# Start-up of a fused retention and MLP kernel: v's first cast on ScalarE, g zeroed and loaded later, fillers cut short, a quarter of w1 loaded earlier

## The chip, the cores and the metric

The kernel runs on one core of a Trainium2 chip. The metric is the device time of one execution in microseconds (us), as the median of several. Most executions of one kernel agree within some 0.3%. Experiments were timed in five rounds beside the kernel before, on the same chip; two were only looked at with a profile. What is discussed is the ratio and its 95% interval. A run is called slow when it is over 1.5% above the fastest of its kernel.

## The reference

```python
# attention part, B, H, S, D = 4, 8, 768, 64
gamma = 1.0 - 2.0 ** (-5.0 - np.arange(H))
for t in range(S):
    state = gamma * state + einsum('bhd,bhe->bhde', k[:, :, t], v[:, :, t])
    y[:, :, t] = scale * einsum('bhd,bhde->bhe', q[:, :, t], state)
x = y.transpose(0, 2, 1, 3).reshape(B, S, H * D)          # 4 x 768 x 512
# MLP part
xn = (x - mean(x)) / sqrt(var(x) + 1e-6) * g_ln
out = x + maximum(xn @ w_ch1, 0) @ w_ch2                  # w_ch1 512 x 2048, w_ch2 2048 x 512
```

## The kernel before

The four sequences are cut into 24 tiles of 128 positions. In the texts below, q(1) is q of tile 1, py(0) the output of tile 0, and so on; g is `g_ln` of the reference, which is needed on all 128 partitions. For a tile, TensorE transposes k and q ("tk", "tq"), makes the scores ("pa") and the output ("py"). VectorE masks the scores and normalises the output to xn. TensorE transposes xn ("tx") and multiplies it by w1 in four quarters for each of the first tiles ("products", line 589); ScalarE or VectorE applies the ReLU. The second matrix product (line 626) follows much later.

A planner inside the kernel decides the order on each engine when the program is built. It holds an estimated duration for each task and takes the task that can start earliest, then the one of lowest rank. Its numbers are estimates that set an order; the chip then runs that fixed order, each engine waiting where data are not there.

The parts that the change touches:

```python
    def c_small(eng):
        nc.vector.memset(zeros, 0.0)
        nc.vector.memset(grow, 0.0)          # 128 x 512, only row 0 is then loaded
        ...
    small = a(DVE, 1450, -100, c_small)      # engine, ns, rank, what to emit
    ...
    maskd = a(DVE, 1230, -50, c_mask, [vscd, tri])
    ...
    def c_gb(eng):                           # g on all partitions: ones^T x grow
        p = take("mm", "g", [P, DM], FP32)
        nc.tensor.matmul(p, lhsT=ones, rhs=grow, start=True, stop=True)

    grd = a(SP, 390, -150, lambda eng: nc.sync.dma_start(
        out=grow[0:1, :], in_=moe_g_ln.rearrange("(o n) -> o n", o=1)), [small], lat=4500)
    gbm = a(PE, 1000, 12, c_gb, [grd, small2], ("mm", "g"), at=7600)
    ...
            if j == 0:                       # tile 0 comes as fp32 and is cast
                loaded[kind, j] = a({"k": {ACT: 620}, "q": {DVE: 490}, "v": {ACT: 620, DVE: 430}}[kind], ...)
    ...
    # GpSimd issues the other loads; a load waits for the one eight places ahead of it
    first = ["iota", "pos", "k1", "q1", "v1", "w1_0", "k2", "q2", "w1_1", "v2", "k3", "q3", "v3",
             "w1_2", "k4", "q4", "v4", "w1_3", "k5", "q5", "v5"]
    ...
    def warm(n):                             # fillers: matmuls on zeros while TensorE would idle
        if ("mm", "warm") not in held:
            take("mm", "warm", [P, GMAX * P], FP32)      # pool "mm" has two buffers
        for w in [GMAX * P] * (n // GMAX) + [P] * (n % GMAX):
            nc.tensor.matmul(held["mm", "warm"][:, 0:w], lhsT=zeros[:, 0:P], rhs=zeros[:, 0:w], ...)
    ...
        for t in plan.fill(plan.order(), PE, 1100, 20000, lambda at: 110 if at < 11500 else 80, warm):
            t["emit"](t["eng"])              # fillers up to 20000 planned ns
```

Of the kernel before, what the change touches and what calls it, by code (L numbers as in the profile page):

```python
# [14 lines left out]
PE, ACT, DVE, POOL, SP = range(5)  # L15
# [101 lines left out]
def kernel(  # L117
# [16 lines left out]
    nc = tc.nc  # L134
# [25 lines left out]
    plan = Plan({PE: 330, ACT: 130, DVE: 130, POOL: 130, SP: 0},  # L160
                {PE: 900, ACT: 800, DVE: 900, POOL: 850, SP: 800}, 2300, 8, 5300)
# [21 lines left out]
    def take(pool, key, shape, dtype):  # L183
        held[pool, key] = pools[pool].tile(shape, dtype, name=pool, tag=pool)
        return held[pool, key]

    def evacuate(eng, dst, src):
        nc.scalar.copy(out=dst, in_=src) if eng == ACT else nc.vector.tensor_copy(out=dst, in_=src)
# [18 lines left out]
    pos = const.tile([P, C, H], FP32, name="pos")  # L207
# [3 lines left out]
    grow = const.tile([P, DM], FP32, name="grow")  # L211
# [5 lines left out]
    w2 = const.tile([P, HO, DM], BF16, name="w2")  # L217
    x_all = const.tile([P, NT, DM], BF16, name="x_all")

    def c_small(eng):  # L220
        nc.vector.memset(zeros, 0.0)  # L221
        nc.vector.memset(grow, 0.0)
        for i in range(NPAIR):
            nc.vector.memset(lgq[0:D, i:i + 1], lngam[2 * i])
            nc.vector.memset(lgq[D:P, i:i + 1], lngam[2 * i + 1])
        nc.vector.memset(ln8, math.log(scale))
        for h in range(H):
            nc.vector.memset(lgh[:, :, h], lngam[h])
# [43 lines left out]
            nc.gpsimd.memset(x, 0.0)  # L272

    a = plan.add
    small = a(DVE, 1450, -100, c_small)
    small2 = a(DVE, 200, -99, c_small2)
    iota = a(POOL, 250, 0, c_iota)
    ipos = a(POOL, 250, 0, c_pos)
# [14 lines left out]
    def c_gb(eng):  # L293
# [1 line left out]
        nc.tensor.matmul(p, lhsT=ones, rhs=grow, start=True, stop=True)  # L295

    grd = a(SP, 390, -150, lambda eng: nc.sync.dma_start(
        out=grow[0:1, :], in_=moe_g_ln.rearrange("(o n) -> o n", o=1)), [small], lat=4500)
    gbm = a(PE, 1000, 12, c_gb, [grd, small2], ("mm", "g"), at=7600)
    gl = a(ACT, 600, -40, lambda eng: nc.scalar.copy(out=gb, in_=held["mm", "g"]), [gbm],  # L300
           uses=[("mm", "g")])
# [3 lines left out]
    loaded, where = {}, {}  # L305

    def tile_of(kind, t):
        if kind != "v" and t >= T0:
            return held["qk", t][:, "qk".index(kind)]
        return held[where[kind, t]]  # L310

    def load(kind, j, rank):
        takes, uses, follows = None, [], []
        if kind in "qkv":
            b, c = TILES[j]
            src = {"q": q, "k": k, "v": v}[kind][b].rearrange("h (c p) d -> c p h d", p=P)[c]
            ns, dma = 910, 900
            pair = kind != "v" and j >= T0
            name = "qk" if pair else kind + ("0" if c == 0 and kind != "q" else "sb")
            takes = where[kind, j] = (name, j)  # L320
            if pair and kind == "q":
                takes, uses, follows = None, [takes], [loaded["k", j]]

            if j == 0:

                def emit32(eng):
                    dst = take("osb", kind, [P, DM], FP32).rearrange("p (h d) -> p h d", d=D)
                    (nc.scalar if eng == ACT else nc.sync).dma_start(out=dst, in_=src)
                raw = a(ACT if kind == "q" else SP, 390, -200 + "kqv".index(kind), emit32, (),
                        ("osb", kind), (), 0, {"k": 3400, "q": 4000, "v": 4800}[kind])  # L330

                def emit(eng):
                    evacuate(eng, take(*takes, [P, H, D], BF16),
                             held["osb", kind].rearrange("p (h d) -> p h d", d=D))
                loaded[kind, j] = a({"k": {ACT: 620}, "q": {DVE: 490}, "v": {ACT: 620, DVE: 430}}[kind], 0, -60, emit,
                                    [raw], takes, [("osb", kind)])
                return

            def emit(eng):
                if takes:  # L340
                    take(*takes, [P, 2, H, D] if pair else [P, H, D], BF16)
                nc.gpsimd.dma_start(out=tile_of(kind, j), in_=src)  # L342
        else:
            s = slice(j * DM, (j + 1) * DM)
            o = slice(j * KO, (j + 1) * KO)
            src, dst = (w1_v[:, :, s], w1[:, :, s]) if kind == "w1" else (w2_v[:, o, :], w2[:, o, :])
            ns, dma = 820, 2450 if kind == "w1" else 2800

            def emit(eng):
                nc.gpsimd.dma_start(out=dst, in_=src)  # L350
        loaded[kind, j] = a(POOL, ns, rank, emit, (), takes, uses, dma,
                            4000 if kind in "qkv" and j > 7 else 1400 if late(kind, j) else 500,
                            follows=follows)

    def late(kind, j):
        return j > 2 if kind in "qkv" else kind == "w2" or j > 0


    first = ["iota", "pos", "k1", "q1", "v1", "w1_0", "k2", "q2", "w1_1", "v2", "k3", "q3", "v3",
             "w1_2", "k4", "q4", "v4", "w1_3", "k5", "q5", "v5"]  # L360
    pool_rank = {x: i - 1000 for i, x in enumerate(first)}
    seq = [(x, t) for t in range(8) for x in "kqv"] + [("w1", j) for j in range(4)]
    seq += [("w2", j) for j in range(4)] + [(x, 8) for x in "kqv"]
# [1 line left out]
    for i, (x, j) in enumerate(seq):  # L365
        load(x, j, pool_rank.get(f"{x}_{j}" if x[0] == "w" else f"{x}{j}", 20 * i))
# [25 lines left out]
    for t in range(NT):  # L392
        b, c = TILES[t]
# [97 lines left out]
        if c > 0:  # L491
            for cc in ([0, 1] if c == 1 else [c]):
                if cc == C - 1:
                    continue
                j = number[b, cc]

                def e_vg(eng, j=j, cc=cc):
                    e = nc.gpsimd if eng == POOL else nc.vector
                    e.tensor_tensor(  # L499
                        out=take("vg", j, [P, H, D], BF16), in0=tile_of("v", j),  # L500
                        in1=vsc[:, cc, :].unsqueeze(2).to_broadcast([P, H, D]), op=ALU.mult)
                vgt = a(POOL, 1050, -500 if j == 4 else r - 2 if cc == 0 else r + 1, e_vg,
                        [loaded["v", j], vscd] + vgs[-1:], ("vg", j), [where["v", j]],
                        lat=2500 if j > 7 else 0,
                        follows=[loaded["q", j + 2]] if T0 <= j < NT - 2 else [])
                vgs.append(vgt)

                def e_pd(eng, j=j, b=b, cc=cc):
                    if cc == 0:
                        take("pd", b, [P, NPAIR, P], FP32)  # L510
                    for i in range(NPAIR):
                        nc.tensor.matmul(  # L512
                            held["pd", b][:, i, :], lhsT=tile_of("k", j)[:, 2 * i:2 * i + 2, :],
                            rhs=held["vg", j][:, 2 * i:2 * i + 2, :],
                            start=(cc == 0 and i == 0), stop=(cc == C - 2), skip_group_check=True)
                pdt = a(PE, 230, r - 1 if cc == 0 else r + 2.2, e_pd,
                        [vgt, loaded["k", j]] + ([pbt[j]] if cc else []),
                        ("pd", b) if cc == 0 else None,
                        [("vg", j), where["k", j]] + ([("pd", b)] if cc else []), at=0 if cc or b else 20000)

                def e_pb(eng, n=number[b, cc + 1], b=b, cc=cc):

                    held["pb", n] = state[len(pbs) % 2]
                    pbs.append(n)
                    for o in (slice(0, D), slice(D, P)):
                        nc.vector.tensor_tensor(  # L526
                            out=held["pb", n][o, :, o], in0=held["pd", b][o, :, o],
                            in1=gch[o, cc, :].unsqueeze(2).to_broadcast([D, NPAIR, D]), op=ALU.mult)
                pbt[number[b, cc + 1]] = a(
                    DVE, 690, r - 1 if cc == 0 else r + 4, e_pb, [pdt, gchd, zerod],  # L530
                    ("pb", number[b, cc + 1]), [("pd", b)])
                if cc == 0:

                    pyt["after"].append(pbt[t])
# [43 lines left out]
    for g in range(NG):  # L578
        n = GROUPS[g]
        hb, h0 = buf_of[g]  # L580
        two = GMAX // n
        for ho in range(0, HO, two):
# [22 lines left out]
            first = ho == 0 and h0 == 0  # L605
# [45 lines left out]
                             start=True, stop=True)  # L651

    with tc.manual_schedule():
        for t in plan.fill(plan.order(), PE, 1100, 20000, lambda at: 110 if at < 11500 else 80, warm):
            t["emit"](t["eng"])


# [28 lines left out]
```

## Time and profile before

| | kernel before |
|---|---|
| median of 3 runs | 215.68 us (215.56 to 215.99) |
| span in the profile | 213.7 us |
| TensorE busy | 96% of the span, 7.95 us of it fillers |
| VectorE, ScalarE, GpSimd busy | 57%, 38%, 42% |
| first product starts | 13.56 us |

In a profile line of the timeline the columns are: start, length (both us), engine, source line, operation with output and inputs, count, and in brackets the idle time just ahead of it with what ended it. One more reading of the kernel before, from VectorE's timeline:

```profile
6.83 0.43 DVE L188 CAST v<-osb 128x512 bf16<-128x512 f32 x1 [0.74 <-DMA osb<-in_v_dram]
7.17 0.42 DVE L416 TENSOR_TENSOR trq<-tp,qsc 128x512 bf16<-128x512 bf16 x1
```

The first part of the change aims at this cast.

### The profile page before, as it was taken

The numbers are of one execution on the slowest core, as the hardware profiler recorded it, in microseconds if no ns is written. First come the engines' busy times: TensorE is split into PE (matmuls) and PEld (weight loads), VectorE is DVE, ScalarE is ACT, GpSimd is POOL, SyncE is SP. The second block draws the span as 40 slices with busy tenths as digits, with TensorE's granted clock in tenths as the row PEclk, the third lists the DMA queues.
The fourth block names the chain that finished last, engine by engine and source line by source line (L and its number), as shares of the span: only waits on it lengthen the run. The fifth ranks groups of instructions, "written<-read, shape, count | busy, mean of one in ns | idle before, by whom it ended". The sixth has DMA issues, their size and how long they took to land.

```text
span 213.7 us, 4698 instructions
## 1 busy us (share of the span) xinstructions
PE 204.9 (96%) x1945; PEld 132.3 (62%) x1966; DVE 121.3 (57%) x235; ACT 80.9 (38%) x152; POOL 89.5 (42%) x105
## 2 busy tenths in 40 slices
PE   7788999999999999999999999999999999999994
PEld 2557999996466456777877785454444444444442
DVE  7685878970745989987872878893511111012121
ACT  5445655673042202645654253145740044430000
POOL 8988789926498296764933830000000000000000
PEclk9999999999999999999999999999999999999999
DMA  7999999999999999999999999720121111011212
GB/s 140 180 179 180 181 157 189 172 184 156 130 203 191 135 243 183 141 171 127 178 140 140 127 176 163 196 81 0 27 71 52 49 49 49 0 52 49 98 49 98
DMA packets 109382, 27.17 MB, mean 127 GB/s; under 512 B 102065, under 2 KB 106417, under 8 KB 109362
## 3 DMA queue, kind: packets, MB, share of 16 engines
q0 software_dynamic: 75984, 13.24, 90.2%
q1 hardware_dynamic: 32194, 13.31, 34.4%
q10 hardware_dynamic: 1184, 0.33, 0.7%
q8 instruction: 15, 0.25, 0.5%
q14 instruction: 5, 0.04, 0.1%
HBM read 27.27 MB, written 6.29 MB: 157 GB/s over the span
## 4 chain that ended last, share of the span: by engine, by line
PE 92%; DMA 3%; DVE 1%; issue 1%; POOL 1%; ACT 1%; POOLq 0%; DVEq 0%
PE mm L589 40%; PE tp L626 39%; PE pa L443 3%; DMA qsb<-in_q_dram 3%; PE py L466 3%; PE pd L512 2%; PE py L462 2%; PE tp L542 1%; PE tp L411 1%; ACT h L602 1%; PE mm L650 1%; POOL k L342 0%; PE tp L403 0%; PE mm L295 0%; DVE xn L475 0%
## 5 line engine op out<-in xcount | busy, mean ns | idle before, releaser
L589 PE MATMUL mm<-xnt,w 128*128 128x128 bf16 (+2 forms) x896 | 93.7, 257 | 0.9 <-ACT h L602 0.9
L626 PE MATMUL tp<-w,h 128*128 128x512 bf16 (+2 forms) x381 | 86.7, 370 | 1.2 <-issue 0.3
L602 ACT ACTIVATE h<-mm 128x512 bf16<-128x512 f32 x88 | 52.5, 597 | 71.0 <-PE mm L589 60.1
L589 PEld LDWEIGHTS <-w 128*128 128x128 bf16 x896 | 65.8, 98 | 19.6 <-issue 1.1
L626 PEld LDWEIGHTS <-h 128*128 128x128 bf16 x400 | 37.3, 98 | 38.8
L634 DVE SCALAR_TENSOR_TENSOR osb<-tp,rstd,x_all 128x512 f32<-128x512 f32 (+2 forms) x25 | 18.2, 728 | 57.3 <-PE tp L626 57.1
L450 DVE TENSOR_TENSOR asb<-pa,mask 128x1024 bf16<-128x1024 f32 x24 | 29.3, 1220 | 9.6 <-PE pa L443 9.5
L480 DVE BATCH_NORM_STATS2 bns<-py 128x6 f32<-128x512 f32 x24 | 16.7, 696 | 14.7 <-PE py L466 14.5
L499 POOL TENSOR_TENSOR vg<-vsb,vsc 128x512 bf16<-128x512 bf16 x16 | 16.9, 1057 | 12.7 <-DMA vsb<-in_v_dram 11.7
L486 ACT CAST x_all<-py 128x512 bf16<-128x512 f32 x24 | 14.0, 584 | 19.1 <-DVE xn L475 19.0
L342 POOL DMA_DIRECT2D qk<-in_k_dram x17 | 15.2, 893 | 14.3 <-DMA tr<-qk 10.7
L342 POOL DMA_DIRECT2D vsb<-in_v_dram x20 | 18.5, 923 | 1.2 <-DMA v<-in_v_dram 0.7
L475 DVE SCALAR_TENSOR_TENSOR xn<-py,mv,gb 128x512 bf16<-128x512 f32 x24 | 18.0, 751 | 0.9
L526 DVE TENSOR_TENSOR state<-pd,gch 64x256 bf16<-64x256 f32 x40 | 16.7, 417 | 0.3
L342 POOL DMA_DIRECT2D qk<-in_q_dram x17 | 15.2, 894 | 2.7 <-DMA w<-in_moe_w_ch_dram 2.7
L650 PE MATMUL mm<-zeros 128*128 128x128 bf16 (+1 forms) x34 | 7.9, 362 | 1.5 <-DVE zeros L221 1.2
L433 DVE TENSOR_TENSOR trq<-tr,qsc 128x512 bf16<-128x512 bf16 x17 | 7.9, 465 | 0.9 <-DMA tr<-qk 0.8
L564 ACT ACTIVATE rstd<-mv,epsb 128x1 f32<-128x1 f32 (+2 forms) x14 | 3.7, 289 | 11.8 <-DVE mv L481 11.8
L466 PEld LDWEIGHTS <-asb 128*128 128x128 bf16 x192 | 7.9, 98 | 0.3 <-DVE trq L416 0.3
L462 PEld LDWEIGHTS <-trq 128*128 128x128 bf16 x80 | 6.0, 98 | 3.2
L466 PE MATMUL py<-vsb,asb 128*128 128x64 bf16 x160 | 7.9, 193 | 0.0
L462 PE MATMUL py<-state,trq 128*128 128x128 bf16 x80 | 7.7, 219 | 0.1
(65 smaller groups left out, 109.3 us busy)
## 6 DMA issues: line engine op xcount, KB each, us to landing
out_dram<-osb SPq DMA_DIRECT2D x23, 256.0 KB, 3.3
w<-in_moe_w_ch_dram POOLq DMA_DIRECT2D x8, 512.0 KB, 10.5
vsb<-in_v_dram POOLq DMA_DIRECT2D x20, 128.0 KB, 8.7
qk<-in_k_dram POOLq DMA_DIRECT2D x17, 128.0 KB, 9.1
qk<-in_q_dram POOLq DMA_DIRECT2D x17, 128.0 KB, 9.7
qsb<-in_q_dram POOLq DMA_DIRECT2D x6, 128.0 KB, 8.9
k<-in_k_dram POOLq DMA_DIRECT2D x3, 128.0 KB, 7.4
v<-in_v_dram POOLq DMA_DIRECT2D x3, 128.0 KB, 9.0
```

The lines of the kernel that those rows point to most:

```text
L342: nc.gpsimd.dma_start(out=tile_of(kind, j), in_=src)
L450: nc.vector.tensor_tensor(out=take("asb", t, [P, NPAIR, 2, P], BF16).rearrange("p i a t -> p a i t"), in0=held["pa", t], in1=mask.rearrang ...
L462: nc.tensor.matmul(py[:, 2 * i:2 * i + 2, :], lhsT=held["trq", t][:, i, :], rhs=held["pb", t][:, i, :], start=(mi == 0), stop=False)
L466: nc.tensor.matmul(py[:, h, :], lhsT=held["asb", t][:, h // 2, h % 2, :], rhs=tile_of("v", t)[:, h, :], start=(mi == 0), stop=(mi == n - 1))
L475: nc.vector.scalar_tensor_tensor(out=take("xn", t, [P, DM], BF16), in0=held["py", t].rearrange("p h d -> p (h d)"), scalar=mv[:, t, 0:1], ...
L480: nc.vector.bn_stats(out=bns[:, t, :], in_=held["py", t].rearrange("p h d -> p (h d)"))
L499: e.tensor_tensor(out=take("vg", j, [P, H, D], BF16), in0=tile_of("v", j), in1=vsc[:, cc, :].unsqueeze(2).to_broadcast([P, H, D]), op=ALU. ...
L526: nc.vector.tensor_tensor(out=held["pb", n][o, :, o], in0=held["pd", b][o, :, o], in1=gch[o, cc, :].unsqueeze(2).to_broadcast([D, NPAIR, D ...
L589: nc.tensor.matmul(p[:, j, :], lhsT=w1[:, ko, (ho + j) * P:(ho + j + 1) * P], rhs=held["xnt", hb][:, h0:h0 + n, ko, :], start=(ko == 0), s ...
L602: nc.scalar.activation(out=dst, in_=src, func=AF.Relu)
L626: nc.tensor.matmul(held[key], lhsT=held["h1", hb][:, ho, i * P:(i + 1) * P], rhs=w2[:, ho, cols], start=(ho == 0), stop=(ho == HO - 1))
L634: nc.vector.scalar_tensor_tensor(out=take("osb", key, [P, w], FP32), in0=held[key], scalar=rstd[:, t:t + 1], in1=x_all[:, t, cols], op0=AL ...
```

## The change

The intent is to shorten the start-up: free VectorE from the cast of v and from a memset that stands ahead of the mask, let products of w1's third quarter start sooner, and stop the fillers when real products begin.

```diff
-        nc.vector.memset(grow, 0.0)
...
-    small = a(DVE, 1450, -100, c_small)
+    small = a(DVE, 1200, -100, c_small)
+    growz = a(DVE, 480, -49, lambda eng: nc.vector.memset(grow, 0.0))
...
     grd = a(SP, 390, -150, lambda eng: nc.sync.dma_start(
-        out=grow[0:1, :], in_=moe_g_ln.rearrange("(o n) -> o n", o=1)), [small], lat=4500)
+        out=grow[0:1, :], in_=moe_g_ln.rearrange("(o n) -> o n", o=1)), [growz], lat=2300)
...
-        ("osb", kind), (), 0, {"k": 3400, "q": 4000, "v": 4800}[kind])
+        ("osb", kind), (), 0, {"k": 3400, "q": 4000, "v": 5200}[kind])
...
-    ... "v": {ACT: 620, DVE: 430}}[kind], ...
+    ... "v": {ACT: 620}}[kind], ...
...
-        return j > 2 if kind in "qkv" else kind == "w2" or j > 0
+        return j > 2 if kind in "qkv" else kind == "w2" or j > 1
...
-    first = [... "k3", "q3", "v3", "w1_2", "k4", "q4", "v4", "w1_3", "k5", "q5", "v5"]
+    first = [... "k3", "q3", "w1_2", "v3", "k4", "v4", "q4", "w1_3", "k5", "v5", "q5"]
...
-        ... at=0 if cc or b else 20000)          # state product of sequence 0
+        ... at=0 if cc or b else 19000)
...
-        for t in plan.fill(plan.order(), PE, 1100, 20000, ...
+        for t in plan.fill(plan.order(), PE, 1100, 14000, ...
```

In what follows, part 1 is the cast of v, part 2 the memset and load of g, part 3 the load order with the belief about w1's second quarter, part 4 the fillers. The earlier planned start of the state product (19000) belongs to none of them.

More of the change, by code (lines that the diff above doesn't have):

```diff
@@ L334, in emit @@
                              held["osb", kind].rearrange("p (h d) -> p h d", d=D))
-                loaded[kind, j] = a({"k": {ACT: 620}, "q": {DVE: 490}, "v": {ACT: 620, DVE: 430}}[kind], 0, -60, emit,
+                loaded[kind, j] = a({"k": {ACT: 620}, "q": {DVE: 490}, "v": {ACT: 620}}[kind], 0, -60, emit,
                                     [raw], takes, [("osb", kind)])
@@ L355, in late @@
     def late(kind, j):
-        return j > 2 if kind in "qkv" else kind == "w2" or j > 0
-    first = ["iota", "pos", "k1", "q1", "v1", "w1_0", "k2", "q2", "w1_1", "v2", "k3", "q3", "v3",
-             "w1_2", "k4", "q4", "v4", "w1_3", "k5", "q5", "v5"]
+        return j > 2 if kind in "qkv" else kind == "w2" or j > 1
+    first = ["iota", "pos", "k1", "q1", "v1", "w1_0", "k2", "q2", "w1_1", "v2", "k3", "q3", "w1_2",
+             "v3", "k4", "v4", "q4", "w1_3", "k5", "v5", "q5"]
     pool_rank = {x: i - 1000 for i, x in enumerate(first)}
@@ L518 @@
                         ("pd", b) if cc == 0 else None,
-                        [("vg", j), where["k", j]] + ([("pd", b)] if cc else []), at=0 if cc or b else 20000)
+                        [("vg", j), where["k", j]] + ([("pd", b)] if cc else []), at=0 if cc or b else 19000)
                 def e_pb(eng, n=number[b, cc + 1], b=b, cc=cc):
@@ L653 @@
     with tc.manual_schedule():
-        for t in plan.fill(plan.order(), PE, 1100, 20000, lambda at: 110 if at < 11500 else 80, warm):
+        for t in plan.fill(plan.order(), PE, 1100, 14000, lambda at: 110 if at < 11500 else 80, warm):
             t["emit"](t["eng"])
```

## The prediction

> **What bounds the kernel now.** I read the span by stretches first, cutting it where the character changes. Columns: stretch, length, TensorE (PE) busy time with instructions, granted clock, DMA share, GB/s.
>
> ```profile
> 5.00:10.00 5.00, 3.97 (x42) 1.00 1.89 180
> 10.00:13.70 3.70, 2.79 (x46) 1.00 1.78 182
> 13.70:25.30 11.60, 10.25 (x182) 1.00 1.85 180
> 25.30:60.00 34.70, 34.59 (x515) 1.00 1.97 169
> 60.00:150.00 90.00, 89.14 (x869) 1.00 1.66 150
> 150.00:210.70 60.70, 60.39 (x302) 1.00 0.15 52
> ```
>
> From 25.3 to 210.7 us TensorE idles 0.11 + 0.86 + 0.31 = 1.3 us. The change removes none of that work, so a gain must come from earlier. The same query for the warm-up matmuls ("fillers", line 650, on zeros) shows what their busy time hides:
>
> ```profile
> 5.00:10.00 5.00, 1.63 (x10) 1.00 1.89 180
> 10.00:13.70 3.70, 1.31 (x7) 1.00 1.78 182
> 13.70:25.30 11.60, 1.21 (x10) 1.00 1.85 180
> ```
>
> Between 5 and 13.7 us idle plus filler is 1.03 + 1.63 + 0.91 + 1.31 = 4.9 us; between 13.7 and 25.3 it is 1.35 + 1.21 = 2.6 us. Only these 7.5 us can be won. What holds them? The chain that ended last, in order of time, at the start (start, length, what):
>
> ```profile
> 2.43 6.16 DMA qsb<-in_q_dram
> 8.59 0.05 issue
> 8.64 0.40 PE tp L411 x4
> 9.03 0.91 PE mm L295 x2
> 9.95 0.06 PE mm L650
> 10.00 0.25 PE py L466 x8
> ```
>
> Tile 1's q lands at 8.59; TensorE, in program order, transposes it (line 411), broadcasts g (line 295), and only then starts tile 0's output (py, line 466). The critical event of the first 10 us is a transfer. Farther on, in the timeline of TensorE:
>
> ```profile
> 16.02 1.06 PE L589 MATMUL mm<-xnt,w 128*128 128x128 bf16 x16
> 16.91 0.40 PE L466 MATMUL py<-v,asb 128*128 128x64 bf16 x8
> 17.76 1.05 PE L589 MATMUL mm<-xnt,w 128*128 128x128 bf16 x16 [0.45 <-ACT h L602]
> 18.65 0.39 PE L403 MATMUL tp<-idn,k 128*128 128x128 bf16 x4
> 19.50 1.05 PE L589 MATMUL mm<-xnt,w 128*128 128x128 bf16 x16 [0.46 <-ACT h L602]
> 20.39 0.39 PE L411 MATMUL tp<-idn,qsb 128*128 128x128 bf16 x4
> 20.61 0.33 PE L650 MATMUL mm<-zeros 128*128 128x128 bf16 x3
> ```
>
> Each product (16 matmuls of line 589) waits for the ReLU (line 602) of the product just before it, as if pool mm had one buffer; it has two. The source says why: the fillers take a tile of mm once and use it up to the last of them, at 20.61. From 22.07 two products run back to back. **The fillers cost more by the buffer they hold than by their time.**
>
> **What the Trainium skill says.** "TensorE: Matmul & The Clock Gate", Part 1, warns that an idle stretch of about 3.4 us halves TensorE's clock; fillers exist for that. The clock column reads 1.00 throughout, so no run here shows it yet; the longest gap that I expect after the change is 1.2 us. The same page, "Phases on the wall clock", has 55.6 ns per 128-column matmul back to back: here 16 take 0.89 us in the chain, 56 ns each. "ScalarE: Activation LUTs", "What ACT_TABLE_LOAD costs", gives 186 ns + 0.833 ns per element with immediate operands, 613 ns for 512; the cast of k took 0.62 us. "DMA: Bandwidth & Descriptors", "Queues, rings and completion order", says that each DMA engine alternates between queues by packets, so a small transfer on SyncE's queue shouldn't sit behind all of GpSimd's loads. Its own time isn't in the page of before.
>
> **The change, part by part.**
>
> 1. *v of tile 0 on ScalarE.* VectorE's cast (6.83, 0.43 us) stands before trq (line 416, at 7.17), though the transposes for trq end at 6.54. ScalarE is free from 6.54 to 8.41. So trq starts near 6.65, scores pa near 7.1 instead of 7.64, the masked product asb ends near 8.75 instead of 9.30. But py(0) stands after q(1)'s transposes and the g broadcast in the order. I worked the order out by hand from the planner's rule (earliest start, then rank): the broadcast may start at 8130 in planned ns, py(0) at 9180, so it stays so. q(1) still lands at 8.59, and py(0) starts at 10.0. **Gain here: 0 to 0.1 us.**
>
> 2. *grow zeroed after the mask.* The 0.48 us memset leaves the front of VectorE's queue; the mask ends near 5.0, the memset takes 5.0 to 5.5, and q(0)'s cast, bound by its landing (0.74 + 4.8 = 5.54), is where it was. g's transfer is issued near 5.6 instead of 1.91; g is needed at 9.03, which leaves 3.4 us for issue and landing. The 192 KB store took 1.9 us in a quiet stretch; v of 256 KB took 5.5 in a busy one. I expect about 2.5 us, hidden. **0 us**, with a risk of some 0.3.
>
> 3. *Third quarter of w1 ahead of v of tile 3.* One query per transfer gives the landings: q(3) 18.5, v(3) 20.4, w1's third quarter 22.5. Swapped I estimate 20.7 for the quarter and 22.5 for v(3). Products of that quarter, begun at 24.4 before, could then start near 21.5. v(3) is needed by py(3), near 23. The planner also believes w1's second quarter 900 ns sooner (15330 instead of 16230 planned ns; it landed at 6.68 + 8.9 = 15.6).
>
> 4. *No fillers after 14 us of the plan.* The last then run near 13 us. This takes away 0.55 + 0.33 + 0.33 us of fillers, most of which lay in real waits, and frees the second mm buffer: the two waits (0.45 and 0.46) and the ReLU's place in the chain go.
>
> Parts 3 and 4 act on 13.7 to 25.3. The order changes there too: py(1) now precedes q(2)'s transposes, so VectorE takes tile 1's statistics before q(2)'s product. My walk, with durations of the trace: first product 13.73 to 14.62, as before; xn(1) done 15.25, its transposes 15.3 (15.65 before); second product 15.65 (w1 lands) to 16.55; pa(2) 16.88; two products to 18.67 with no wait; py(2), two transposes and pd(0) to 19.56; **a wait for VectorE's statistics and xn(2) to 20.7**; transposes and pa(3) to 21.45; two products of the third quarter to 23.25; py(3) and k(4)'s transposes to 23.7; product to 24.6. The same seven products and py(3) were done at 25.31. So 25.31 - 24.6 = **0.7 us**. TensorE is full from there, so this carries to the end: 215.68 - 0.7 = 215.0. I take 215.0 us.
>
> **Rivals.**
>
> - *The transfers hold everything.* For: DMA share 1.8 to 2.0 up to 60 us; q(1), k(2), q(2) and w1's second quarter land just when wanted. Against: products did wait for ReLUs, not loads, at 17.8 and 19.5. If it governs all: within 0.2 us of before, 215.5 to 215.9.
> - *The new order favours tile 1 over tile 2.* pa(2) comes near 16.6 instead of 14.6, so tile 2's chain becomes the wait at 19.6 to 20.7. That is in my number. If the planner kept q(2)'s product first, the same walk gives about 24.0 at the seventh product: gain 1.3, 214.4.
> - *g comes late.* Each us of landing after 9.03 delays py(0) as much; perhaps 0.3 us, and the gain shrinks to 0.4.
> - *The fixed order of the rest is drawn anew.* Only 1.3 us of idle is left after 25.3, so it can hardly get better and may get worse by some 0.3 us. q(4) and q(5) load after v(4) and v(5), a us later each; products should fill the holes.
> - *The fillers' own time is the gain* (1.2 us at once): against it, the 0.55 us at 15.1 ends where xn(1) ends, so that part saves nothing.
>
> **Range and chances.** Largest plausible gain 1.3 + 0.4 for luck in the order: 214.0. Worst: no gain and a new wait of 0.2: 215.9. The 8-in-10 range is 214.0 to 215.9. Two per cent is 4.3 us. A gain of that needs most of the 7.5 us that were open, over half of them before the first product and tied to the landing at 8.59; a loss of that needs a wait nothing here points to. Faster 0.01, same 0.98, slower 0.01.
>
> **What would show it.** py(0) within 0.1 us of 10.0, behind line 295, with trq of tile 0 near 6.65: part 1 moved VectorE and not the chain. No line-650 matmul after about 13.5 and no product waiting for the ReLU just before it: part 4. Granted clock 1.00. The seventh product ending near 24.6, with a TensorE gap of about 1.1 us near 20: the walk. Fillers' total down from 7.95 to about 6.5. Idle after 25.3 still near 1.3 us. The prediction fails if g lands after 9.1, if q(1) lands elsewhere than 8.6, if VectorE's order at 13.5 isn't mine, or if new waits show after 25.3.

## The result

The changed kernel takes 216.0 us (median of 4, 215.9 to 216.44) against 215.72 us before (4 runs). The ratio is 1.0016, with an interval of 0.9998 to 1.0033. All runs were with a granted clock of 1.00. A ratio, here and below, is the mean time of one kernel's fast runs over that of the other's of the same rounds, so it is not quite the ratio of the medians quoted. The expected gain of 0.7 us is not there, and the time lies just outside the range of 214.0 to 215.9.

The stretches of the changed kernel, with the same cuts and columns as in the prediction (TensorE alone):

```profile
5.00:10.00 5.00, 2.84 (x35) 1.00 1.88 180
13.70:25.30 11.60, 9.66 (x177) 1.00 1.85 180
25.30:60.00 34.70, 34.49 (x524) 1.00 1.86 161
60.00:150.00 90.00, 89.16 (x867) 1.00 1.60 153
```

From 25.3 us on it is much as full as before (idle 1.3 us up to 210.7, as predicted). Between 5 and 10 us TensorE is busy 2.84 us instead of 3.97. The chain that ended last, at the start (start, length, what):

```profile
5.34 4.55 DMA grow<-in_moe_g_ln_dram
9.93 1.12 PE mm L295 x2
11.05 0.25 PE py L466 x8
```

In the kernel before, this stretch of the chain ran through the load of tile 1's q, which landed at 8.59. Now it runs through the load of g, issued at 5.34 and landed at 9.89. The broadcast of g starts at 9.93 instead of 9.03, and the output of tile 0 at 11.05 instead of 10.00. TensorE's timeline shows the same from its side, and what followed:

```profile
9.93 1.12 PE L295 MATMUL mm<-grow,ones 128*128 128x512 f32 x2 [0.90 <-DMA grow<-in_moe_g_ln_dram]
18.05 1.96 PE L589 MATMUL mm<-xnt,w 128*128 128x128 bf16 x32
22.04 0.40 PE L542 MATMUL tp<-idn,xn 128*128 128x128 bf16 x4 [1.13 <-DVE xn L475]
```

TensorE stood 0.90 us for a row of 2 KB. The line at 18.05 is two products without a wait between them, so the buffer that the fillers held was free, as predicted. The line at 22.04 is the predicted wait for VectorE's statistics; 1.13 us against the 1.14 us of the walk. Fillers came to 6.60 us where about 6.5 was forecast, but with the whole start a microsecond late some still ran at 13.73, and the seventh product ended near 26.0, not 24.6. VectorE did gain:

```profile
6.65 0.42 DVE L416 TENSOR_TENSOR trq<-tp,qsc 128x512 bf16<-128x512 bf16 x1 [0.56 <-PE tp L411]
```

This is the 6.65 of the prediction, against 7.17 before, and it reached nothing, because py(0) waits for something else.

### The profile page after: what moved, and what is told of

The parts are those of the page before. It is cut to its first block, busy times and chain, and to the rows that moved or that the text cites. A ratio compares the mean times of both kernels' runs of the same rounds, so it can differ in the third digit from the quotient of the medians.

```text
span 214.3 us, 4674 instructions
## 1 busy us (share of the span) xinstructions
PE 203.7 (95%) x1934; PEld 131.4 (61%) x1956; DVE 120.7 (56%) x233; ACT 82.7 (39%) x154; POOL 89.3 (42%) x105
## 4 chain that ended last, share of the span: by engine, by line
PE 91%; DVE 4%; DMA 2%; issue 1%; ACT 1%; DVEq 0%; ACTq 0%
PE mm L589 40%; PE tp L626 38%; PE pa L443 3%; PE py L466 3%; DMA grow<-in_moe_g_ln_dram 2%; PE py L462 2%; PE pd L512 2%; PE tp L542 1%; DVE xn L475 1%; DVE bns L480 1%; DVE mask L261 1%; PE mm L295 1%; PE tp L411 0%; PE tp L403 0%; ACT h L602 0%
## 5 line engine op out<-in xcount | busy, mean ns | idle before, releaser
L589 PE MATMUL mm<-xnt,w 128*128 128x128 bf16 (+2 forms) x896 | 94.0, 257 | 0.0
L589 PEld LDWEIGHTS <-w 128*128 128x128 bf16 x896 | 65.5, 98 | 19.4
L499 POOL TENSOR_TENSOR vg<-vsb,vsc 128x512 bf16<-128x512 bf16 x16 | 16.9, 1058 | 12.2 <-DMA vsb<-in_v_dram 10.7
L650 PE MATMUL mm<-zeros 128*128 128x512 bf16 (+1 forms) x25 | 6.6, 389 | 1.4 <-DVE zeros L221 1.2
```

The costliest lines, as they stand in the source:

```text
L499: e.tensor_tensor(out=take("vg", j, [P, H, D], BF16), in0=tile_of("v", j), in1=vsc[:, cc, :].unsqueeze(2).to_broadcast([P, H, D]), op=ALU. ...
L589: nc.tensor.matmul(p[:, j, :], lhsT=w1[:, ko, (ho + j) * P:(ho + j + 1) * P], rhs=held["xnt", hb][:, h0:h0 + n, ko, :], start=(ko == 0), s ...
```

## Experiments

Lines are numbered by each run's own kernel; in one_row_g, which has one line less, L588 is the L589 of the others. Theory A: the load of g ate the gain. Theory B: later loads and the new order hold the kernel, and the late g is absorbed by waits that come anyway. The first four kernels ran on one chip in five rounds (kernel before: 215.51 us, 11 runs).

### g_early: the change with part 2 undone, every order kept

```diff
         nc.vector.memset(zeros, 0.0)
+        nc.vector.memset(grow, 0.0)
...
-    growz = a(DVE, 480, -49, ...)
-    ... [growz], lat=2300)
-    gbm = a(PE, 1000, 12, c_gb, [grd, small2], ("mm", "g"), at=7600)
+    ... [small], lat=4500)
+    gbm = a(PE, 1000, 12, c_gb, [grd, small2], ("mm", "g"), at=8130)
```

The 8130 is the planned start of the broadcast in the changed kernel; without it the planner would have moved the broadcast ahead of tile 1's q. The duration of `small` goes back to 1450 too.

> The changed kernel with one thing undone: grow is zeroed at the front of VectorE's queue and its row loaded near 1.9 us again, while every engine's order stays that of the changed kernel (g's broadcast stays after q of tile 1). Theory A (the load of g landing at 9.9 us instead of before 9.0 holds TensorE and is all that ate the gain): no wait of line 295 for the load of grow, py of tile 0 starts near 10.0 instead of 10.9, first product near 13.75 instead of 14.92, time 1.0 us below the changed kernel, near 215.0, which is the 0.7 us below the kernel before that was predicted. Theory B (later loads and the new order hold the kernel, the late g is absorbed by waits that come anyway): within 0.3 us of the changed kernel, near 216.0.

Measured: 215.36 us, ratio 0.9989 (0.9976 to 1.0002). That is some 0.25 us below before, where 0.7 was expected, and the interval just holds no gain at all. In its timeline py of tile 0 starts at 9.75, the first product at 13.62, and there is no wait for g. TensorE:

```profile
20.91 0.40 PE L542 MATMUL tp<-idn,xn 128*128 128x128 bf16 x4 [1.13 <-DVE xn L475]
23.83 1.95 PE L589 MATMUL mm<-xnt,w 128*128 128x128 bf16 x32
27.84 1.96 PE L589 MATMUL mm<-xnt,w 128*128 128x128 bf16 x32 [0.17 <-DMA w<-in_moe_w_ch_dram]
```

The seventh product, and the pair of the tenth and eleventh, in the kernel before:

```profile
24.25 1.06 PE L589 MATMUL mm<-xnt,w 128*128 128x128 bf16 x16
28.04 1.95 PE L589 MATMUL mm<-xnt,w 128*128 128x128 bf16 x32
```

Three things follow. The start was restored, so theory A holds for it. The walk of the prediction had the right order and the right waits, but was some 0.3 us short: the seventh product is the first of the pair at 23.83, against 24.25 before, so with the same 1.06 us it ends near 24.9, where 24.6 was predicted and before has 25.31. The lead there is 0.4 us, not 0.7. And then comes a wait that the walk did not reach. In this order the first product that needs the fourth quarter of w1 stands at 27.84. Its chain shows that load landing at 27.79 and the state product after the pair at 29.80; before, that pair ended at 29.99. A lead of 0.4 us had become 0.2.

Beside the changed kernel's 1.0016 the ratio is lower by 0.0027, some 0.6 us, with an uncertainty of about 0.5 us (the two were timed on different chips); the spans in the profiles, 214.3 and 213.7, differ by as much. So the late g did not eat all of the gain in the changed kernel, as theory A had it: the rest, some 0.45 us, is missing with g early too.

### g_late_alone: the kernel before with part 2 alone

The edit is the part of the change's diff that concerns `growz`, `small` and `grd`. Every engine's order is that of before, save for the memset.

> The kernel before with part 2 alone: grow zeroed and loaded behind the mask, every order as before. Theory A: g lands near 9.9, py of tile 0 starts near 11.0 instead of 10.0, first product near 14.7, and the time is 0.8 to 1.1 us above before, near 216.6. Theory B: the delay is absorbed by the waits up to 22 us and the time is within 0.3 us of before.

Measured: 216.48 us, ratio 1.0053 (1.0035 to 1.0072), so 1.1 us slower. The late g is not absorbed in this order. Theory B falls for the start.

Its profile was taken of the slowest of the six executions (217.77 us; the other five lie between 216.3 and 216.67). It shows something else, in stretches of one us (TensorE busy, then granted clock):

```profile
8.00:9.00 1.00, 0.71 (x8) 1.00 1.40 190
9.00:10.00 1.00, 0.21 (x1) 0.95 1.24 208
10.00:11.00 1.00, 1.00 (x2) 0.50 1.75 175
```

After the wait for g, which is 0.79 us long here, the clock dropped to half until about 13.3 us. That execution is therefore no measure of the load alone. The ratio counts it as one of six; the other five, at a granted clock of 0.999 to 1.00, lie some 0.9 us above before. The changed kernel has the same wait and kept its clock in all four runs.

### fillers_alone: the kernel before with part 4 alone

```diff
-        for t in plan.fill(plan.order(), PE, 1100, 20000, ...
+        for t in plan.fill(plan.order(), PE, 1100, 14000, ...
```

> The kernel before with part 4 alone: no fillers after 14000 planned ns, orders otherwise as before. Theory A (the warm tile held one of the two buffers of mm until 20.6 us): the two waits of a product for the ReLU just before it (0.45 and 0.46) vanish, the seventh product ends near 24.5 instead of 25.3, time 0.5 to 0.9 us below before, near 215.0; granted clock stays 1.00. Rival (the buffer does not matter, only the fillers' own time): at most 0.3 us below before. Rival (without fillers the clock drops): slower.

Measured: 214.6 us, ratio 0.9964 (0.9952 to 0.9976), 0.8 us faster; clock 1.00. TensorE:

```profile
16.63 0.41 PE L466 MATMUL py<-v,asb 128*128 128x64 bf16 x8
16.87 1.06 PE L589 MATMUL mm<-xnt,w 128*128 128x128 bf16 x16
17.77 0.39 PE L403 MATMUL tp<-idn,k 128*128 128x128 bf16 x4
17.99 1.06 PE L589 MATMUL mm<-xnt,w 128*128 128x128 bf16 x16
23.10 0.40 PE L403 MATMUL tp<-idn,ksb 128*128 128x128 bf16 x4 [0.41 <-DMA ksb<-in_k_dram]
```

The same two products started at 17.76 and 19.50 before, each behind a ReLU. Now they start at 16.87 and 17.99 with no wait. From the second product to the fourth it now takes 2.26 us (15.73 to 17.99) instead of 3.48 (16.02 to 19.50), and no filler stood between them before. So the buffer was the cause, and not the fillers' own time. This part alone is worth about what the whole change was predicted to bring. Part of the lead is given back at 23.10, where k of tile 4 has not landed: 1.51 us at the pair before it (20.49 against 22.00), 0.92 at the seventh product (23.33 against 24.25).

### v_alone: the kernel before with part 1 alone

```diff
-    ... {"k": 3400, "q": 4000, "v": 4800} ... "v": {ACT: 620, DVE: 430}
+    ... {"k": 3400, "q": 4000, "v": 5200} ... "v": {ACT: 620}
-    gbm = ... at=7600)
+    gbm = ... at=8130)
```

> The kernel before with part 1 alone (v of tile 0 cast by ScalarE), g's broadcast held behind q of tile 1 as in the kernel before. Expected by the prediction: trq of tile 0 starts near 6.65 instead of 7.17, py of tile 0 still near 10.0 because q of tile 1 lands at 8.6, so the first product within 0.1 us of 13.73; the planner puts py of tile 1 ahead of q of tile 2 and so favours tile 1, which may move the time by 0.3 us either way: 215.4 to 216.0. Rival (VectorE was the bound of the start): 0.5 us below before.

Measured: 215.48 us, ratio 0.9999 (0.9987 to 1.0011). trq starts at 6.64. From the start of tile 1's q transposes to py(0) it takes as long as before:

```profile
8.36 0.40 PE L411 MATMUL tp<-idn,qsb 128*128 128x128 bf16 x4 [0.51 <-DMA qsb<-in_q_dram]
9.57 0.40 PE L466 MATMUL py<-v,asb 128*128 128x64 bf16 x8
```

That is 9.57 - 8.36 = 1.21 us, against 9.84 - 8.64 = 1.20 before; only the landing itself differs by 0.3 us between the two profiles. Moving half a microsecond of VectorE bought nothing while a transfer decides.

### w1_alone: the kernel before with part 3 alone

The edit is the part of the change's diff that concerns `late` and `first`. This kernel, g_early_w3_late, g_late_other_queue and one_row_g ran on another chip (kernel before: 215.72 us, 9 runs).

> The kernel before with part 3 alone: third quarter of w1 ahead of v of tile 3, v ahead of q for tiles 4 and 5, second quarter believed 900 ns sooner; fillers to 20 us, so the warm tile still holds a buffer of mm. The prediction gave this part products of the third quarter near 21.5 instead of 24.4, but no gain of its own. The planner now puts tile 0's second product ahead of tile 1's transposes, and the fourth quarter's first product behind the ninth product: I expect a wait for w1's second quarter near 15 us and one for the fourth near 27.5, and no gain: 215.5 to 216.2. Rival (the earlier quarter is what makes the window shorter): 0.4 us or more below before.

Measured: 215.5 us, ratio 0.9993 (0.9981 to 1.0006): no gain that can be told from none. The two waits for w1 that I had expected, near 15 and 27.5 us, did not show; in this profile q of tile 3 was waited for instead, 0.43 us at 19.50.

### g_early_w3_late: is it the fourth quarter of w1?

g_early with one planner number changed, so that the first product of the fourth quarter comes one product later.

```diff
-                            4000 if kind in "qkv" and j > 7 else 1400 if late(kind, j) else 500,
+                            ... else 2200 if (kind, j) == ("w1", 3) else 1400 if late(kind, j) else 500,
```

> The kernel of g_early with one planner number changed: the fourth quarter of w1 is believed 800 ns later, so that the first product that needs it (line 589, at 27.84 in g_early, waiting for that load) comes behind tile 3's first product, as in the kernel before. Every order up to 27.3 us stays. Theory (g_early was 0.6 us ahead of before at the ninth product and lost 0.4 us of it at 27.3 to 27.8 to the landing of that quarter): no wait for w1 near 27.8, state product (line 462) of tile 4 starts near 29.2 instead of 29.64, time 0.3 to 0.4 us below g_early, near 214.9. Rival (g_early's gain was lost elsewhere, after 30 us): same as g_early, 215.3.

Measured: 215.19 us, ratio 0.9978 (0.9966 to 0.9991). g_early had 0.9989 on another chip. TensorE has no wait for w1 any more; the pair of products starts at 27.68 right behind the scores:

```profile
27.68 1.96 PE L589 MATMUL mm<-xnt,w 128*128 128x128 bf16 x32
```

The difference, 0.11% or 0.24 us, has the right sign and about two thirds of the size expected, but the intervals of the two ratios overlap. The expectation had read the lead at the ninth product as 0.6 us; it was 0.4 (26.28 against 26.49, with the 0.22 us of "pd" already done), of which the wait took 0.2, and that is the size measured. The trace shows the wait gone; that the whole loss after the walk was this wait is likely, and not shown by the times alone.

### g_late_other_queue and g_issued_later: what sets the landing of g?

The first issues the row from ScalarE's queue instead of SyncE's; the second keeps SyncE and zeroes grow behind trq of tile 0, so that the row is issued 2.3 us later. The second ran on a third chip.

```diff
-    grd = a(SP, 390, -150, lambda eng: nc.sync.dma_start(          # g_late_other_queue
+    grd = a(ACT, 390, -150, lambda eng: nc.scalar.dma_start(
```

```diff
-    growz = a(DVE, 480, -49, lambda eng: nc.vector.memset(grow, 0.0))            # g_issued_later
+    growz = a(DVE, 480, -49, lambda eng: nc.vector.memset(grow, 0.0), at=6930)
-    ... [growz], lat=2300) ... at=7600)
+    ... [growz], lat=300) ... at=8130)
```

> The changed kernel with the row of g issued from ScalarE's queue, near 5.5 us, instead of SyncE's, at 5.34. Theory A (the row waits at the DMA engine for GpSimd's loads, whatever queue it is in): it lands near 9.9 again and line 295 waits about 0.9 us for it. Theory B (the row waits behind v of tile 0 in SyncE's own queue): ScalarE's queue is empty by 5.6, so it lands 2 to 2.5 us after issue, near 8, and line 295 does not wait.

> The changed kernel with grow zeroed behind trq of tile 0, so that its row is issued near 7.6 us instead of 5.34 (on SyncE's queue again; the planner's figure for its latency is lowered so that the order stays). A wrong place for it on purpose, to see what sets its landing. Theory A1 (it waits until GpSimd's loads that were queued by then let it through, near 9.6): it lands within 0.5 us of 9.9 again, 2.3 us after issue. Theory A2 (each load at this stage takes some 4.5 us from its own issue, as it waits behind what was queued before it): it lands near 12.1, line 295 waits about 3 us, and TensorE's clock may drop.

The chain of g_late_other_queue (216.36 us) at the start:

```profile
5.34 4.47 DMA grow<-in_moe_g_ln_dram
9.86 1.12 PE mm L295 x2
```

The chain of g_issued_later (220.88 us):

```profile
7.64 4.51 DMA grow<-in_moe_g_ln_dram
12.29 2.04 PE mm L295 x2
```

Four measurements of one row of 2 KB: 4.55, 4.41 (g_late_alone), 4.47 and 4.51 us, in two queues and at two times of issue. So it is not a matter of the queue, and not of one moment at which GpSimd's loads let it through: in this stretch such a row takes some 4.5 us from its own issue. GpSimd's loads took 6 to 9 us each in the same stretch. What inside the DMA engines takes the time, these traces do not tell. In the second kernel TensorE stood 3.08 us, and its clock was at half from about 10.7 to 17.5 us, so its broadcast took 2.04 us instead of 1.12; its time is therefore no measure of the late load alone.

### one_row_g and fillers_and_k4: towards a version that beats both

fillers_and_k4 ran on the third chip (kernel before: 215.52 us, 11 runs). one_row_g is the changed kernel with g in one partition. Nothing has to be zeroed, so the load is issued early; the broadcast multiplies one row of ones by one row of g.

```diff
-    grow = const.tile([P, DM], FP32, name="grow")
+    grow = const.tile([1, DM], FP32, name="grow")
-        nc.tensor.matmul(p, lhsT=ones, rhs=grow, start=True, stop=True)
+        nc.tensor.matmul(p, lhsT=ones[0:1, :], rhs=grow, start=True, stop=True)
-    growz = a(DVE, 480, -49, ...)
-    ... out=grow[0:1, :] ... [growz], lat=2300)
+    ... out=grow ... (), lat=5200)
-        return ... or j > 1
+        return ... or j > 0
```

> A version meant to beat both: the changed kernel with g held in one partition (the broadcast multiplies one row of ones by one row of g, so nothing has to be zeroed and the load is issued near 1.9), g's broadcast ahead of q of tile 1, and w1's second quarter believed as late as before, so that scores of tile 2 come ahead of tile 0's second product. If the broadcast of one row costs what that of 128 did (0.91 us in the chain), py of tile 0 starts near 9.4 instead of 10.0, and the window up to 25 us is at least as short as in fillers_alone (eighth product done near 25): 214.3 to 214.7. If the window is held by loads (second quarter of w1 at 15.5, k of tile 4 at 23.1), the earlier start is lost and the time is that of fillers_alone, 214.6.

Measured: 214.95 us, ratio 0.9968 (0.9954 to 0.9981), as good as fillers_alone within the intervals, on another chip. The 214.3 to 214.7 of its expectation was missed. TensorE:

```profile
9.25 0.40 PE L465 MATMUL py<-v,asb 128*128 128x64 bf16 x8
21.22 1.96 PE L588 MATMUL mm<-xnt,w 128*128 128x128 bf16 x32 [0.87 <-DMA w<-in_moe_w_ch_dram]
```

py(0) starts half a microsecond earlier, and at 21.22 TensorE stands 0.87 us for w1's third quarter. The earlier start was turned into a wait for a load, which is theory B at a later place. The broadcast of one row was no cheaper than that of 128: its two instructions took 1.12 us here and 1.08 us in g_early.

fillers_and_k4 is fillers_alone with two planner numbers, to fill the wait at 23.10.

```diff
-                            ... else 1400 if late(kind, j) else 500,
+                            ... else 2200 if (kind, j) == ("w1", 3) else 1900 if (kind, j) == ("k", 4)
+                            else 1400 if late(kind, j) else 500,
```

> The best so far, fillers_alone (214.6), with two planner numbers: k of tile 4 believed 500 ns later and w1's fourth quarter 800 ns later, so that tile 0's third product fills the 0.41 us for which k of tile 4 was waited for at 23.1, and no product of the fourth quarter comes before 28. If that wait was on the path: 0.3 to 0.5 us below fillers_alone, near 214.2 (1.2 to 1.4 below before). If the products of the third quarter (its load lands near 22.1) or tile 3's statistics take the wait's place: 214.6, as fillers_alone.

Measured: 216.54 us (216.05 to 217.63, 6 runs), ratio 1.0043 (1.0019 to 1.0066), about 1.7 us worse than fillers_alone. Its profile, of its slowest execution, has no wait for k of tile 4, but among others this one:

```profile
58.54 1.02 PE L626 MATMUL tp<-w,h 128*128 128x512 bf16 x4 [0.72 <-DVE osb L634]
```

A miss. The two numbers drew the order anew far beyond the place that they were meant for. How the loss is shared out among the new waits was not settled.

**The version that beats both** is fillers_alone: one number of the change, 0.36% below the kernel before in the same rounds. one_row_g is level with it.

## Why the prediction was wrong

**The step that failed is part 2 of the sum** (g zeroed and loaded later), "about 2.5 us, hidden", with "0 us" for its cost. The row took 4.55 us from its issue at 5.34 and landed at 9.89, where 9.03 was needed. Alone it costs 0.53%, 1.1 us; in the changed kernel some 0.6 us of the 1.0 us between prediction and measurement (g_early). The estimate went between a store of 192 KB in a quiet stretch, 1.9 us, and the first load of v, of 256 KB, 5.5 us, as if size set the time. But that load of v, issued at 1.27, had GpSimd's loads in flight around it and the store had not, and the same profile has loads of 128 KB that took 6 to 9 us at that stage. The prediction named the mechanism as a rival, "g comes late", and gave it "perhaps 0.3 us". What that rival would cost per us was about right: g landed 0.86 us after 9.03, and py(0) started 1.05 us later.

**A second step was too large: the 0.7 us of the walk, and "this carries to the end".** With g early the wait for xn(2) was 1.13 us, as walked, but the seventh product ended near 24.9, so the lead was 0.4 us. The walk counted 1.79 us for each pair of products. A pair behind scores takes 0.1 us more in the chain, 1.89 us at 21.72 in g_early_w3_late and also in the kernel before, where the prediction could have read it, and there are two such pairs on the way. The pair in the kernel before:

```profile
22.07 1.89 PE mm L589 x32
```

Then the lead of 0.4 us ran into the landing of w1's fourth quarter at 27.79, and g_early kept only 0.11%, about 0.25 us. "TensorE is full from there" was read from the kernel before, whose order has another product at that place.

**Part 1 was right.** trq moved to 6.65 and py(0) did not follow; alone it gives 0.9999.

**Part 3 was right in giving no gain of its own**; alone it gives 0.9993, not distinguishable from 1. What it did inside the changed order was not measured apart. The third quarter landed at 21.4 there, not at the 20.7 of the prediction, and nothing waited for it.

**Part 4 was right in mechanism and too modest in the sum.** The warm tile held a buffer of mm; free of it, two products lost their waits. Alone it gives 0.9964, 0.8 us. The prediction credited parts 3 and 4 together with 0.7 us. Together, with part 1's order, they gave 0.25 us (g_early), so the rest of the change cost about half a microsecond of what the fillers' end brought. Which part of it did is not shown.

**The ledger closes within its noise.** The four parts alone add up to -0.0001 (v) + 0.0053 (g) - 0.0007 (w1) - 0.0036 (fillers) = +0.0009; the change measured +0.0016, with an interval that holds both. Adding is only a rough check: the sum of four ratios is itself uncertain by about 0.003, 0.6 us, and each part also moves the order. The late g cost 1.1 us alone and some 0.6 us in the changed kernel.

**The clock** stayed at 1.00 in the changed kernel, as predicted. It is less safe than the prediction thought: a wait of 0.79 us went with a drop to half in one execution of six of g_late_alone.

## What to carry to other kernels

Before a small load is moved later, read how long loads of any size take from issue to landing at the stage where it will be issued, not at another; size says little there (2 KB took some 4.5 us where 128 KB took 7.2 to 7.4). A scratch tile taken from a rotating pool holds one of its buffers until its last use, so look at what waits for what before counting only the scratch work's own time. And a lead won early is worth only what the next transfer lets through: follow the walk past the place where TensorE is full, to the next load that an earlier order will have to wait for.

## What the Trainium skill lacked or had wrong

- "DMA: Bandwidth & Descriptors", "Queues, rings and completion order", describes taking turns between queues by packets, from which I concluded, and the page does not state, that a small transfer is not held up much by another queue's loads. Here one row of 2 KB took 4.41 to 4.55 us from issue to landing while GpSimd's loads were in flight, on SyncE's and on ScalarE's queue alike. The page's fixed cost of about 2 us, in "Anatomy of one DMA", is given for GpSimd's path, and what else was in flight is not said; in "Latency and other measured facts" it adds only that HBM access takes 2 us at high load instead of 0.2. A figure for a small transfer among other loads is lacking.
- "TensorE: Matmul & The Clock Gate", Part 1, ties the drop to half clock to an idle window of about 3.4 us. In one execution of six of g_late_alone it dropped at about 9.9 us, after a gap of 0.79 us; the us before was 71% busy. The half clock then lasted some 3.4 us, which agrees with the page's window, and in g_issued_later some 6.8 us. In the changed kernel a gap of 0.90 us did not drop it in four runs. Part 1 also tells of a kernel whose clock fell from short idles between groups of matmuls, but gives no length for them; a figure is lacking.
